# A hand-ordered kernel for RWKV6 attention and a squared-ReLU MoE: a new order, four shared banks, fp32 dummy products

## The chip, the cores and the metric

The kernel runs on one core of one Trainium2 chip. The metric is the device time of one execution in microseconds (us); smaller is better. The core has five engines that work at the same time and are tied by semaphores: TensorE (PE, with its weight loads as PEld), VectorE (DVE), ScalarE (ACT), GpSimd (POOL) and SyncE (SP), which here only issues DMAs. Each engine takes its instructions strictly in the order in which the program gives them.

## The reference

Inputs `r`, `k`, `v`, `w` have shape (4, 8, 768, 48): batch, heads, sequence, head size. `u` is (8, 48), `moe_w_in` is (384, 2048), `moe_w_out` is (2048, 384).

```python
state = zeros((B, H, D, D))
for t in range(S):
    cur   = einsum('bhd,bhe->bhde', u * k[t], v[t])
    y[t]  = einsum('bhd,bhde->bhe', r[t], state + cur)
    state = w[t][..., None] * state + einsum('bhd,bhe->bhde', k[t], v[t])
x   = y.transpose(0, 2, 1, 3).reshape(B * S, H * D)     # (3072, 384)
h   = maximum(x @ w_in, 0)
out = (h * h) @ w_out                                   # (3072, 384)
```

## The kernel before

The 3072 tokens are cut into 12 steps of 256 tokens, three for each of the four sequences. Step `s` does the recurrence for its tokens in two chunks (numbered `c` or 0 and 1) and then the two MoE products for the same tokens.

The attention of a step: `ld` loads w, k, r and v (384 KB each, line 178, on SP's queue). `ww_` (line 264), `kw_` (290) and `rw_` (286) are products with the decay; `lw_` (268) takes a logarithm; `cum_` (324 to 328) sums it on TensorE, `exp_` (340) and `ac_` (346) exponentiate it; `rd_` (358 and 361, always VectorE) makes decayed r and k. Their transposes come from TensorE (`tr_`, line 374, copied by `rkt_`, 389 and 392) for steps 0 to 3 and from DMA (`dtr_`, 401 and 403) for steps 4 to 11. `p_` (420) multiplies them in 64x64 tiles of the array, `pm_` (431 or 434, VectorE) masks the result; `su_` (446), `ts_` (454, 456) and `sn_` (461, POOL) carry the state; `yc_` (493) and `y_` (483) make the output; `ku_` (297), `qp_` (302), `q_` (307), `qs_` and `vs_` (277) and `vq_` (316) make the term with `u`; `ysb_` (504, VectorE) adds all up. `p_`, `su_` and `yc_` use 64x64 tiles of the TensorE array, all other products the whole 128x128 array. `ts_` is a copy for the first chunk of a sequence, on the engine that its word names; for all others it is an addition on VectorE, whatever the word names.

The MoE of a step: `yt_` (516) and `xt_` (521), or a DMA (`dyt_`, 525) from step 6 on, transpose the sum; `m1_` (536) is one of eight parts of the first product, six matmuls of 128x256; `rl_` (545 on ACT, 547 on DVE) is the ReLU, `sq_` (553 or 555) the square; `m2_` (561) is a quarter of the second product for one chunk, four matmuls of 128x384; `os_` (568 or 570) scales, and `store` (574) writes 192 KB. The weights come in eight loads of 768 KB (lines 188 and 194, `ld.g.i` and `ld.g.o`) and `cast` (200) makes them bf16.

The order of everything is the text `ORDER` (lines 17 to 93): one word for one operation, and each engine gets its share of the words in the order in which they stand. `=A`, `=V`, `=G` name ACT, DVE or POOL; `:0`, `:1`, `:m`, `:b` and so on name a PSUM bank. PSUM holds two double banks `att` for the attention, two banks `bk` for the second MoE product and for transposes, and two banks `m1` for the first product. `warm_.n.i` is n dummy products of 128x512 with zeros (line 578), whose result nobody reads.

Of the kernel before, what the change touches and what calls it, by code (L numbers as in the profile page):

```python
# [27 lines left out]
m1_.0.5:0 v_.2=A xt_.1=V qp_.2=G sn_.1.1 m1_.0.4:1 rl_.0.5=A p_.2.1:1 su_.2:b sq_.0.0=A rl_.0.4=V ld.2.o
m1_.1.4:0 cast.i.3=G ts_.2.0=V pm_.2.1 m1_.1.5:1 rl_.1.4=A q_.2 sn_.2.0 m1_.1.3:0 rl_.1.5=A ld.3.o vs_.2.1=G
vs_.2.0=A yc_.2.0:0 yc_.2.1:0 rl_.1.3=V m1_.1.6:1 cast.o.0=G qs_.2=A m1_.1.0:0 ld.3.k rl_.1.6=V sq_.0.2=A  # L30
y_.2:0 rl_.1.0=V m1_.1.1:1 vq_.2=G m1_.1.7:0 rl_.1.1=V ld.3.v m2_.0.1.0:0 sq_.1.2=A rl_.1.7=V sq_.0.1=A
cast.o.1=G m1_.1.2:1 rl_.1.2=A ysb_.2=V m1_.0.7:0 ld.4.w ww_.3=G yt_.2:1 rl_.0.7=V m1_.0.6:1 xt_.2=V m2_.0.1.1
sq_.1.1=A rl_.0.6=V ld.5.w m1_.2.6:0 cast.o.2=G lw_.3 sq_.1.0=A rl_.2.6=A cum_.3:1 sq_.1.3=A rw_.3=G al_.3
ld.5.r m2_.0.0.0:1 m1_.2.7:1 m2_.0.0.1 cast.o.3=V exp_.3 sq_.0.3=A ld.4.k rd_.3.0 kw_.3=G m1_.2.1:0 rl_.2.7=A
ac_.3 m2_.0.1.2 m2_.0.0.2 rl_.2.1=V ku_.3=G m2_.0.0.3 rd_.3.1 ld.4.v m2_.0.1.3 vs_.3.0=A m1_.2.0:1 os_.0.1=V
qp_.3=G ld.5.v m1_.2.3:0 os_.0.0=V rl_.2.0=V tr_.3.1:0 rl_.2.3=A tr_.3.0:1 rkt_.3.1=V v_.3=A ld.4.r m1_.2.4:1
ww_.4=G rkt_.3.0=V m2_.1.0.0:0 rl_.2.4=A q_.3 ww_.5=G p_.3.1:0 vs_.3.1=A ld.6.k su_.3:1 pm_.3.1 p_.3.0:m
m2_.1.0.1 ts_.3.0=A lw_.4 sn_.3.0 ld.5.k pm_.3.0 m2_.1.0.2 qs_.3=A m2_.1.1.0:1 sq_.2.0=A vq_.3=G ts_.3.1=V
m2_.1.0.3 ld.6.w cum_.4:0 m2_.1.1.1 ku_.4=G ac_.4 al_.4 store.0.1 m1_.2.5:0 os_.1.0=A v_.5=A yc_.3.1:1 y_.3:1
lw_.5 kw_.4=G m1_.2.2:1 ld.6.r ysb_.3=V rl_.2.5=A m2_.1.1.2 exp_.4 sn_.3.1 rl_.2.2=V yt_.3:0 rw_.4=G cum_.5:1  # L40
xt_.3=V m2_.1.1.3 vs_.4.0=A ac_.5 sq_.2.1=A qp_.4=G al_.5 m1_.3.0:0 rd_.4.1 v_.4=A m1_.3.3:1 rd_.4.0 dtr_.4.1
m2_.2.0.0:0 rl_.3.0=A rw_.5=G rl_.3.3=A m2_.2.0.1 os_.1.1=V exp_.5 q_.4 dtr_.4.0 su_.4:0 sq_.2.2=A m1_.3.4:0
kw_.5=G rd_.5.0 ww_.6=G m2_.2.1.0:1 rl_.3.4=A ts_.4.0=V sq_.2.3=A m1_.3.5:1 vs_.4.1=A rd_.5.1 sn_.4.0
m2_.2.1.1 store.1.0 ts_.4.1=V rl_.3.5=V ku_.5=G m1_.3.6:0 store.1.1 m2_.2.1.2 qs_.4=A ld.7.w ld.6.v rw_.6=G
p_.4.1:1 rl_.3.6=A p_.4.0:0 pm_.4.1 pm_.4.0 m2_.2.1.3 lw_.6 vq_.4=G m1_.3.1:1 m1_.3.2:0 rl_.3.1=A su_.5:1
dtr_.5.1 dtr_.5.0 vs_.5.1=G sq_.3.0=A rl_.3.2=V yc_.4.0:0 yc_.4.1:0 sn_.4.1 y_.4:0 os_.2.1=V sq_.3.1=A
m1_.3.7:1 ysb_.4=V ld.7.v m2_.2.0.2 rl_.3.7=A ld.8.w kw_.6=G vs_.5.0=G yt_.4:1 ld.7.k sq_.3.3=A m2_.2.0.3
xt_.4=V cum_.6:0 al_.6 m1_.4.4:0 qp_.5=G os_.2.0=A ac_.6 m1_.4.7:1 ts_.5.0=V exp_.6 rl_.4.4=V m2_.3.0.0:1
rl_.4.7=A rd_.6.1 m1_.4.6:0 rd_.6.0 m2_.3.0.1 dtr_.6.1 m2_.3.1.0:0 ku_.6=G qp_.6=G sq_.3.2=A rl_.4.6=A q_.5
dtr_.6.0 p_.5.0:1 p_.5.1:0 vs_.6.0=A m1_.4.5:1 sn_.5.0 m2_.3.0.2 qs_.5=G rl_.4.5=A pm_.5.1 pm_.5.0 vq_.5=G  # L50
m1_.4.1:0 m1_.4.3:1 rl_.4.3=A store.2.1 ld.8.v m2_.3.0.3 rl_.4.1=V ld.8.k v_.6=A ww_.7=G y_.5:0 q_.6 os_.3.0=A
ld.7.r m1_.4.0:1 store.0.0 ld.9.k ww_.8=G yc_.5.0:0 qs_.6=A su_.6:1 yc_.5.1:0 ysb_.5=V vs_.6.1=A ts_.6.0=V
m1_.4.2:0 ld.8.r m2_.3.1.1 rl_.4.0=V yt_.5:1 xt_.5=V sn_.6.0 lw_.7 vq_.6=G rl_.4.2=A p_.6.0:0 m2_.3.1.2
sq_.4.3=A store.2.0 pm_.6.0 m1_.5.2:1 ku_.7=G m1_.5.6:0 ts_.6.1=V yc_.6.1:0 sq_.4.0=A rl_.5.2=A p_.6.1:1
rl_.5.6=A m2_.3.1.3 kw_.7=G pm_.6.1 sq_.4.2=A m1_.5.4:1 rw_.7=G m1_.5.3:0 os_.3.1=V rl_.5.4=A y_.6:0 sn_.6.1
rl_.5.3=A cum_.7:1 kw_.8=G ysb_.6=V al_.7 m2_.4.0.0:1 vs_.7.1=A m1_.5.7:1 m1_.5.5:0 v_.7=G dyt_.6 sq_.4.1=A
rl_.5.7=V qp_.7=G rl_.5.5=V m2_.4.1.0:0 exp_.7 ld.9.w ld.9.v m2_.4.0.1 ac_.7 rd_.7.0 sq_.5.1=A m2_.4.0.2
ku_.8=G rd_.7.1 sq_.5.3=A dtr_.7.0 m2_.4.0.3 m1_.5.0:1 lw_.8 m1_.5.1:0 rw_.8=G rl_.5.0=V su_.7:0 q_.7
rl_.5.1=A cum_.8:1 dtr_.7.1 m1_.6.3:1 qs_.7=A m1_.6.5:0 rl_.6.3=V ld.10.w qp_.8=G ac_.8 sq_.5.0=A m2_.4.1.1
os_.4.0=V ts_.7.0=V ld.11.w sn_.7.0 m1_.6.4:1 rl_.6.5=A al_.8 ww_.9=G m2_.4.1.2 ld.9.r rl_.6.4=V exp_.8  # L60
store.3.0 m2_.5.1.0:1 sq_.5.2=A rd_.8.1 ts_.7.1=V sn_.7.1 m1_.6.0:0 vs_.7.0=G vs_.9.1=A rd_.8.0 m2_.4.1.3
m2_.5.1.1 kw_.9=G rl_.6.0=A dtr_.8.0 p_.7.1:0 v_.8=A p_.7.0:1 vq_.7=G pm_.7.1 m1_.6.1:1 m2_.5.1.2 rl_.6.1=A
pm_.7.0 ku_.9=G m2_.5.1.3 sq_.6.0=A lw_.9 m1_.6.6:0 dtr_.8.1 store.3.1 q_.8 yc_.7.0:0 v_.9=A yc_.7.1:0
rl_.6.6=V rw_.9=G su_.8:1 y_.7:0 os_.5.1=A ts_.8.0=V m1_.6.2:1 ysb_.7=V os_.4.1=A cum_.9:1 m1_.6.7:0 al_.9
dyt_.7 m2_.5.0.0:1 rl_.6.2=V exp_.9 ww_.10=G rl_.6.7=V m2_.5.0.1 ac_.9 ld.10.r rd_.9.1 sq_.6.1=A sq_.6.2=A
sn_.8.0 qp_.9=G ld.10.k qs_.8=G store.4.1 m2_.5.0.2 ld.10.v rd_.9.0 m2_.5.0.3 m2_.6.1.0:0 vs_.8.1=G sq_.6.3=A
dtr_.9.0 vs_.8.0=A p_.8.0:m p_.8.1:0 pm_.8.0 su_.9:1 m2_.6.1.1 ts_.9.0=A pm_.8.1 m2_.6.1.2 lw_.10 m1_.7.4:0
# [564 lines left out]
```

## Time and profile before

| what | value |
|---|---|
| time, median of 3 runs | 182.44 us (182.27 to 183.0) |
| span of the profiled execution, first to last instruction | 182.2 us |
| the profiled execution's own time beside its span | not recorded apart; the lowest run, 182.27 us, stands 0.07 us above the span |
| PE busy | 171.8 us, 94% |
| ACT busy | 132.7 us, 73% |
| DVE busy | 130.0 us, 71% |
| POOL busy | 122.7 us, 67% |
| DMA | 35.81 MB, mean 197 GB/s |

A row of a group reads: line, engine, operation, output tile <- input tiles, shapes, count, then the busy time in us and the mean ns of one. A row of the timeline reads: start in us, duration in us, engine, line and operation, and in square brackets the idle time of the engine ahead of it with what ended it. A row of the chain reads: start, duration, what. A row of the windows reads: window, its length, busy us of PE, PEld, DVE, ACT and POOL with instruction counts in brackets, then the granted clock, the DMA share and GB/s. A matmul's duration in the profile includes its way through the array, so matmuls in a row overlap; their price is the distance between starts, which the chain shows.

### The profile page before, as it was taken

To read this page: it belongs to the slowest core of one execution; us is meant where nothing else is said; L and a number is where in the kernel's file an instruction comes from. 1 tells how busy PE (TensorE), PEld (TensorE's weight loads), DVE (VectorE), ACT (ScalarE), POOL (GpSimd) and SP (SyncE) were. 2 spreads that over 40 slices of the span, in tenths; PEclk is the share of its full clock that TensorE was granted. 3 is DMA by queue.
4 is the path that set the end of the run, shared out by engine and by line. 5 is a ranking of instruction groups with operands and counts; after the bars stand their busy time and mean duration, and the time that the engine had idled before them with its cause. 6 is when DMAs were issued, how large, how long until landed. Compare 5 with 4: busy or idle time off the path is not lost.

```text
span 182.2 us, 5695 instructions
## 1 busy us (share of the span) xinstructions
PE 171.8 (94%) x2385; PEld 123.4 (68%) x2385; DVE 130.0 (71%) x195; ACT 132.7 (73%) x235; POOL 122.7 (67%) x140
## 2 busy tenths in 40 slices
...
GB/s 138 263 263 240 221 359 350 337 314 311 234 274 230 261 158 270 99 247 130 239 296 205 193 270 172 252 189 193 171 109 195 150 47 0 86 144 33 0 86 130
DMA packets 79208, 35.81 MB, mean 197 GB/s; under 512 B 72400, under 2 KB 77648, under 8 KB 79184
## 3 DMA queue, kind: packets, MB, share of 16 engines
...
q8 instruction: 18, 0.29, 0.7%
q14 instruction: 6, 0.05, 0.1%
...
## 4 chain that ended last, share of the span: by engine, by line
PE 75%; SPq 10%; DMA 8%; ACT 4%; issue 1%; DVE 1%; ACTq 0%
PE bk L561 32%; PE m L536 32%; SPq L178 8%; DMA w_st<-in_moe_w_in_dram 5%; PE att L420 3%; DMA rT<-rdec_buf 2%; PE att L483 2%; PE att L493 2%; PE att L446 1%; ACT gt L545 1%; PE att L326 1%; ACT wi_sb L200 1%; PE bk L516 1%; SPq L188 1%; SPq L205 1%
## 5 line engine op out<-in xcount | busy, mean ns | idle before, releaser
L536 PE MATMUL m<-xT,wi_sb 128*128 128x256 bf16 x576 | 74.0, 273 | 1.3 <-ACT gt L545 1.2
L561 PE MATMUL bk<-wo_sb,gt 128*128 128x384 bf16 x384 | 71.9, 326 | 0.0
L536 PEld LDWEIGHTS <-wi_sb 128*128 128x128 bf16 x576 | 54.8, 98 | 13.0 <-issue 0.9
L561 PEld LDWEIGHTS <-gt 128*128 128x128 bf16 x384 | 36.9, 98 | 19.2
L545 ACT ACTIVATE gt<-m 128x512 f16<-128x512 f32 x56 | 33.0, 595 | 22.3 <-PE m L536 21.9
L553 ACT ACTIVATE gt<-gt 128x1024 bf16<-128x1024 f16 x42 | 43.3, 1051 | 1.4 <-DVE gt L547 1.1
L547 DVE TENSOR_SCALAR gt<-m 128x512 f16<-128x512 f32 x40 | 27.0, 686 | 9.6 <-PE m L536 9.3
L434 DVE TENSOR_TENSOR pmT<-att,mask 128x1024 bf16<-128x1024 f32 x20 | 23.9, 1218 | 4.5 <-PE att L420 4.5
L297 POOL TENSOR_TENSOR ku<-k_raw,u_bc 128x768 f32<-128x768 f32 x12 | 21.8, 1819 | 0.2 <-DMA u_bc<-in_u_dram 0.2
L302 POOL TENSOR_TENSOR ku<-ku,r_raw 128x768 f32<-128x768 f32 x11 | 20.7, 1881 | 0.2
L316 POOL TENSOR_TENSOR ku<-v_sh,qs 128x768 f32<-128x768 bf16 x11 | 16.3, 1479 | 4.9 <-ACT qs L277 4.8
L277 ACT CAST v_sh<-v_raw 64x384 bf16<-64x384 f32 x34 | 17.3, 508 | 0.4
L290 POOL TENSOR_TENSOR k_raw<-k_raw,w_raw 128x384 f32<-128x384 f32 x12 | 12.2, 1013 | 6.4 <-DMA k_raw<-in_k_dram 6.3
L286 POOL TENSOR_TENSOR r_raw<-r_raw,w_raw 128x384 f32<-128x384 f32 x12 | 12.0, 1000 | 6.4 <-DMA r_raw<-in_r_dram 6.4
L504 DVE TENSOR_TENSOR y_sb<-att,ku 128x768 bf16<-128x768 f32 x12 | 11.4, 953 | 5.5 <-issue 1.6
L461 POOL TENSOR_TENSOR S<-t_state,ac_buf 128x192 bf16<-128x192 f32 x20 | 10.2, 512 | 6.4 <-DVE t_state L456 3.4
L361 DVE TENSOR_TENSOR kdec_buf<-k_raw,att 128x768 bf16<-128x768 f32 x12 | 11.4, 949 | 3.4 <-ACT att L340 2.8
L358 DVE TENSOR_TENSOR rdec_buf<-r_raw,att 128x384 bf16<-128x384 f32 x24 | 12.1, 547 | 2.2 <-ACT att L340 1.1
L340 ACT ACTIVATE att<-att 128x768 f32<-128x768 f32 x12 | 9.6, 798 | 3.1 <-PE att L328 1.9
L568 ACT ACTIVATE o_sb<-bk 128x384 f32<-128x384 f32 x13 | 6.3, 485 | 7.4 <-PE bk L561 7.3
L307 DVE TENSOR_REDUCE q<-ku 128x16 f32<-128x768 f32 x12 | 11.3, 943 | 0.0
L578 PE MATMUL att<-warm 128*128 128x512 bf16 x27 | 9.1, 492 | 1.2 <-DVE half_ones L228 1.2
...
## 6 DMA issues: line engine op xcount, KB each, us to landing
...
rT<-rdec_buf SPq DMA_TRANSPOSE x16, 4.1
```

The lines of the kernel that those rows point to most:

```text
L178: nc.sync.dma_start(out=t[:, hs, at:at + 2, :].rearrange("p h j d -> p h (j d)"), in_=src[b, hs, i * T:(i + 1) * T, :].rearrange("h (p j) ...
L277: copy(out[j * Q:(j + 1) * Q, c], src[c * Q:(c + 1) * Q, :, j])
L290: tensor_mul("kw_", s, h)(raw["k", s][:, hs, 0, :], raw["k", s][:, hs, 1, :], raw["w", s][:, hs, 1, :])
L297: tensor_mul("ku_", s, h)(tiles["ku", s][:, hs], raw["k", s][:, hs, 1:3, :], u_bc[:, hs, None, :].to_broadcast([C, n, 2, D]))
L302: tensor_mul("qp_", s, h)(ku, ku, raw["r", s][:, heads(h), 0:2, :])
L316: tensor_mul("vq_", s)(vq[:], tiles["vs", s][:], tiles["qs", s][:, :, :, None].to_broadcast([C, 2, H, D]))
L434: nc.vector.tensor_mul(pmT, ps_p[:].rearrange("p e (x t) -> p (e x) t", t=C), mk.to_broadcast([C, 8, C]))
L536: nc.tensor.matmul(ps1[:, j, :], wi_sb[:, n // 4, kk, n % 4 * 128:(n % 4 + 1) * 128], tiles["xT", s][:, :, kk, :], start=(kk == 0), stop=( ...
L545: nc.scalar.activation(rl, m1, AF.Relu, scale=RS)
L547: nc.vector.tensor_scalar(out=rl, in0=m1, scalar1=RS, scalar2=0.0, op0=ALU.mult, op1=ALU.max)
L553: nc.scalar.activation(gt, rl, AF.Square)
L561: nc.tensor.matmul(m2, gt[:, n, c * C:(c + 1) * C], wo_sb[:, n, :], start=(n == 0), stop=(n == NT - 1))
```

## The change

Three things change.

1. `ORDER` is written anew. The loads now come as w, k, r, v of step 0, then w, k, r of step 1, `u`, v of step 1, w of step 2, two loads of `moe_w_in`, and then r and k of step 2. The first MoE parts of steps 0 and 1 stand ahead of most of step 2's attention. On TensorE the parts of `p_` and `yc_` of one step are more often apart, with MoE parts between them. Engines are named anew: over the whole kernel `sq_` has 17 words on V instead of 6, `rl_` 32 instead of 40, `kw_` 6 instead of 0, `rw_` 3 instead of 0, `ww_` 4 instead of 2, `ku_` 3 instead of 0, `qp_` 5 instead of 1, `vq_` 5 instead of 1, `vs_` 7 instead of 0, `v_` 1 instead of 0, `xt_` 4 instead of 6, `os_` 9 instead of 11 and `rkt_` 4 instead of 5. The number of loads, stores, matmuls of the real work and DMA transposes stays.
2. The four single banks become one list, `quad`. `m1_` and `m2_` may each use any of the four. The quarters of `m2_` may come in any order: the first to run starts the sum and the last to run ends it.
3. The zeros of the dummies become fp32, and there are 12 of them instead of 46.

The core of the diff, with the opening of `ORDER` up to `yt_.2` in the old and the new form (the rest of the order is left out):

```diff
-ld.0.w ld.0.k ld.0.r ld.0.u ld.1.w ww_.0=V lw_.0 warm_.11.5 cum_.0:0 kw_.0=G exp_.0 rd_.0.1 ld.0.v warm_.8.5
-tr_.0.1:0 rkt_.0.1=A ld.1.k ld.1.r rw_.0=G ld.2.w ku_.0=G rd_.0.0 ld.1.v warm_.3.5 tr_.0.0:1 ww_.1=V
-rkt_.0.0=A qp_.0=V ld.2.r v_.0=A warm_.5.5 p_.0.0:m p_.0.1:1 ac_.0 lw_.1 q_.0 su_.0:b ld.2.k cum_.1:0
-ts_.0.0=A kw_.1=G pm_.0.0 pm_.0.1 vs_.0.0=A sn_.0.0 ld.1.i exp_.1 rw_.1=G vs_.0.1=A qs_.0=A rd_.1.1 ku_.1=G
-warm_.3.2 yc_.0.1:1 ld.0.i ac_.1 ts_.0.1=V rd_.1.0 warm_.2.2 tr_.1.1:0 sn_.0.1 y_.0:1 rkt_.1.1=A vq_.0=V
-tr_.1.0:1 ww_.2=G ld.2.i v_.1=A rkt_.1.0=V ysb_.0=V vs_.1.1=A warm_.4.2 p_.1.1:0 qp_.1=G su_.1:m ld.2.v
-pm_.1.1 lw_.2 yt_.0:0 cum_.2:1 ld.3.i ts_.1.0=V rw_.2=G q_.1 exp_.2 kw_.2=G xt_.0=V vs_.1.0=A rd_.2.0 qs_.1=G
-ac_.2 cast.i.1=A rd_.2.1 warm_.10.1 tr_.2.0:1 sn_.1.0 p_.1.0:0 ku_.2=G ts_.1.1=V yc_.1.1:1 tr_.2.1:0
-cast.i.0=A pm_.1.0 ld.0.o m1_.0.3:0 ld.3.w rkt_.2.1=V m1_.0.2:1 vq_.1=G rkt_.2.0=V y_.1:1 rl_.0.3=A yc_.1.0:1
...
+ld.0.w ww_.0=V lw_.0 warm_.5.4 cum_.0:0 ld.0.k kw_.0=G exp_.0 rd_.0.1 ld.0.r rw_.0=G ac_.0 rd_.0.0 warm_.2.5
+tr_.0.1:2 ld.0.v rkt_.0.1=A v_.0=G tr_.0.0:1 rkt_.0.0=V vs_.0.1=A ld.1.w ww_.1=G lw_.1 su_.0:m p_.0.1:b
+pm_.0.1 vs_.0.0=A p_.0.0:1 pm_.0.0 ld.1.k cum_.1:0 exp_.1 kw_.1=G rd_.1.1 ld.1.r rw_.1=G rd_.1.0 ts_.0.0=A
+sn_.0.0 ld.0.u ku_.0=V qp_.0=V q_.0 ku_.1=G qp_.1=G ts_.0.1=A sn_.0.1 warm_.2.0 tr_.1.1:2 rkt_.1.1=A qs_.0=G
+vq_.0=G yc_.0.1:1 y_.0 ac_.1 tr_.1.0:0 rkt_.1.0=A warm_.1.1 p_.1.0:b pm_.1.0 p_.1.1:0 ld.1.v v_.1=A pm_.1.1
+q_.1 vs_.1.1=A warm_.1.3 su_.1:b ysb_.0=V yc_.1.0:0 ld.2.w ww_.2=V warm_.1.3 yt_.0:3 xt_.0=V vs_.1.0=G
+ts_.1.0=A ld.1.i cast.i.1=A sn_.1.0 ld.0.i ts_.1.1=A y_.1 m1_.0.3:1 yc_.1.1 m1_.0.2:2 qs_.1=A lw_.2 cum_.2:1
+cast.i.0=G m1_.0.1:3 vq_.1=V ysb_.1=V rl_.0.2=A yt_.1:2 xt_.1=V rl_.0.3=V exp_.2 ld.2.r rw_.2=G rd_.2.0 ld.2.k
+m1_.0.0:0 kw_.2=G rd_.2.1 rl_.0.1=A m1_.1.0:3 rl_.0.0=A rl_.1.0=A m1_.1.1:1 rl_.1.1=A sq_.1.0=A sn_.1.1 ld.2.i
+ac_.2 ld.2.v sq_.0.0=A tr_.2.0:3 rkt_.2.0=V cast.i.2=V ku_.2=G v_.2=G tr_.2.1:0 rkt_.2.1=V qp_.2=V ld.3.i
+m1_.1.3:3 rl_.1.3=A m1_.1.4:1 vs_.2.0=G ld.1.o su_.2:0 p_.2.0:1 ts_.2.0=V vs_.2.1=A cast.i.3=G m1_.0.4:2
+sn_.2.0 m1_.1.2:3 p_.2.1:0 ld.0.o m1_.1.5:0 ld.3.w pm_.2.0 rl_.1.4=A rl_.0.4=A m1_.0.5:2 ld.2.o sq_.0.1=A
+ld.3.o m1_.1.6:1 rl_.1.2=V yc_.2.1:1 pm_.2.1 y_.2 rl_.0.5=A sq_.1.1=V m1_.0.6:3 rl_.1.6=V cast.o.1=G m1_.1.7:1
+ld.3.k cast.o.0=G rl_.1.5=V yc_.2.0 rl_.0.6=V q_.2 m1_.0.7:0 sq_.1.2=A m2_.0.1.1:3 m2_.0.1.0 m2_.1.1.1:2
+ld.3.r ww_.3=G qs_.2=A cast.o.3=G rl_.0.7=V m2_.0.0.1:0 cast.o.2=A lw_.3 rl_.1.7=V sq_.0.2=V vq_.2=V m2_.1.1.0
+ysb_.2=V sq_.0.3=V m2_.0.0.0 m2_.0.0.2 yt_.2:1 xt_.2=V ku_.3=G cum_.3:1 al_.3 qp_.3=G m2_.1.1.2 sq_.1.3=A
...
+    quad = bk + m1_bank
...
-    warm = consts.tile([C, 512], BF16)
+    warm = consts.tile([C, 512], FP32)
...
-        ps1 = tiles["m1", s, g] = m1_bank[int(slot["m1_", s, g])][:].rearrange("p (j t) -> p j t", j=2)
+        ps1 = tiles["m1", s, g] = quad[int(slot["m1_", s, g])][:].rearrange("p (j t) -> p j t", j=2)
...
+    summed = {}
+
     def m2_(s, c, q):
         gt = tiles["gt", s]
-        m2 = bk[int(slot["m2_", s, c])][:, 0:DM]
-        for n in range(4 * q, 4 * q + 4):
-            nc.tensor.matmul(m2, gt[:, n, c * C:(c + 1) * C], wo_sb[:, n, :],
-                             start=(n == 0), stop=(n == NT - 1))
+        m2 = quad[int(slot["m2_", s, c])][:, 0:DM]
+        summed[s, c] = summed.get((s, c), 0) + 1
+        for n in range(4):
+            nc.tensor.matmul(m2, gt[:, 4 * q + n, c * C:(c + 1) * C], wo_sb[:, 4 * q + n, :],
+                             start=(summed[s, c] == 1 and n == 0), stop=(summed[s, c] == NT // 4 and n == 3))
...
-            nc.tensor.matmul((bk + m1_bank)[i][:] if i < 4 else att[i - 4][:, 0, :], warm[:, 0:C], warm[:],
+            nc.tensor.matmul(quad[i][:] if i < 4 else att[i - 4][:, 0, :], warm[:, 0:C], warm[:],
                              start=True, stop=True)
```

128 lines of the change are left out of this document (60 added, 68 removed).

## The prediction

> **What bounds the kernel now.** I read the page first, then the windows, the waits of PE, the chain of work that ended last, and last the timeline of DVE in the opening.
>
> ```profile
> span 182.2 us, 5695 instructions
> PE 171.8 (94%) x2385; PEld 123.4 (68%) x2385; DVE 130.0 (71%) x195; ACT 132.7 (73%) x235; POOL 122.7 (67%) x140
> PE 75%; SPq 10%; DMA 8%; ACT 4%; issue 1%; DVE 1%; ACTq 0%
> ```
>
> PE holds three quarters of the chain. Which stretch that is, the windows show (PE, PEld, DVE, ACT, POOL busy):
>
> ```profile
> 42.00:118.60 76.60, 76.05 (x1161) 56.05 (x1159) 63.01 (x96) 65.42 (x117) 66.57 (x70) 1.00 1.10 224
> 100.00:120.00 20.00, 20.00 (x334) 14.54 (x333) 18.20 (x29) 15.74 (x28) 18.14 (x24) 1.00 1.25 228
> ```
>
> From 42 us on PE is busy without a gap (76.05 of 76.60) while DVE is busy 82% of that stretch, and 91% in its fullest 20 us here. PE's own waits are small:
>
> ```profile
> PE m L536 <- ACT gt L545: 1.2, 1, 1.2
> PE att L420 <- DMA rT<-rdec_buf: 0.6, 2, 0.4
> ```
>
> The first MoE product starts here, in PE's timeline:
>
> ```profile
> 26.99 1.47 PE L536 MATMUL m<-xT,wi_sb 128*128 128x256 bf16 x12
> ```
>
> So the kernel is a gapless PE behind an opening of some 27 us with little real PE work in it. The change can win in the opening only, and it can lose in two ways: by more PE time, or by an engine that no longer keeps ahead of PE. The chain gives PE's prices as distances between starts, and three marks in time:
>
> ```profile
> 42.00 0.34 PE bk L516 x6
> 53.63 0.26 PE att L446 x32
> 59.20 0.66 PE m L536 x6
> 59.86 0.65 PE bk L561 x4
> 64.37 0.37 PE att L446 x32
> 64.74 0.76 PE m L536 x6
> 118.58 0.51 PE att L483 x16
> 178.91 0.49 ACT o_sb L568
> ```
>
> The first row is `yt_.2`, the transpose of step 2's sum; the seventh is `y_` of step 8; the last is the last `os_`, after which the store takes the rest of the 182.2 us. A `su_` inside a block of 64x64 work takes 0.26; one that comes straight after a 128x128 product takes 0.37; and an `m1_` after such a block takes 0.76 instead of 0.66. Each block of 64x64 work (a run of `p_`, `su_`, `yc_` with nothing else between) thus costs 0.11 at its entry and 0.10 at its exit, about 0.22 us, whatever is in it.
>
> **The change part by part.** I split the time at `yt_.2`, which waits for `ysb_.2` on DVE in both orders.
>
> (a) The opening, by DVE's queue. Its rows:
>
> ```profile
> 7.73 0.95 DVE L361 TENSOR_TENSOR kdec_buf<-k_raw,att 128x768 bf16<-128x768 f32 x1 [2.60 <-ACT att L340]
> 20.34 0.94 DVE L504 TENSOR_TENSOR y_sb<-att,ku 128x768 bf16<-128x768 f32 x1
> 21.20 1.21 DVE L434 TENSOR_TENSOR pmT<-att,mask 128x1024 bf16<-128x1024 f32 x1
> 33.80 0.69 DVE L547 TENSOR_SCALAR gt<-m 128x512 f16<-128x512 f32 x1 [0.82 <-PE m L536]
> 37.78 1.29 DVE L547 TENSOR_SCALAR gt<-m 128x512 f16<-128x512 f32 x2 [0.43 <-PE m L536]
> 39.42 1.35 DVE L547 TENSOR_SCALAR gt<-m 128x512 f16<-128x512 f32 x2 [0.35 <-PE m L536]
> 40.68 0.95 DVE L504 TENSOR_TENSOR y_sb<-att,ku 128x768 bf16<-128x768 f32 x1
> ```
>
> The last row is `ysb_.2`, done at 41.63; `yt_.2` follows at 42.00. From the first row (`rd_.0.1`) on, DVE's 41 instructions up to there last 31.9 us by their group means; neighbours overlap by 0.07 (0.94 us long, but 20.34 to 21.20 between starts), so 29.0 us without gaps, against 33.9 that passed. DVE idled 4.8 us, 1.6 of it in the three waits for `m1_` shown. In the new order DVE has ahead of `ysb_.2` the same kinds and counts and in addition one `ku_`, one `qp_`, one `vq_`, one `cast`, two `sq_`, and a `pm_` in two halves instead of whole:
>
> ```profile
> L302 DVE TENSOR_TENSOR ku<-ku,r_raw 128x768 f32<-128x768 f32 x1 | 0.9, 945 | 0.0
> L316 DVE TENSOR_TENSOR ku<-v_sh,qs 128x768 f32<-128x768 bf16 x1 | 1.7, 1683 | 0.0
> L200 DVE CAST wo_sb<-w_st 128x1536 bf16<-128x1536 f32 x1 | 1.0, 1031 | 0.1
> L555 DVE TENSOR_TENSOR gt<-gt 128x1024 bf16<-128x1024 f16 x6 | 4.3, 732 | 5.8 <-ACT gt L545 5.7
> L434 DVE TENSOR_TENSOR pmT<-att,mask 128x1024 bf16<-128x1024 f32 x20 | 23.9, 1218 | 4.5 <-PE att L420 4.5
> L431 DVE TENSOR_TENSOR pmT<-m,mask 128x512 bf16<-128x512 f32 x8 | 5.1, 684 | 2.0 <-ACT v_sh L277 1.3 <-PE m L420 0.7
> ```
>
> That is 2 x 0.945 (`ku_` has `qp_`'s shape) + 1.683 + 1.031 + 2 x 0.732 + (2 x 0.684 - 1.218) = 6.2 us, less seven overlaps of 0.07: 5.7 us. DVE now runs behind PE, so I let the three waits for `m1_` go (-1.6) and keep the other 3.2 us of idling. `yt_.2` comes **4.1 us later**, at 46.1. Bounds: -4.8 + 5.7 = +0.9 if DVE never idles, +5.7 if it idles as before.
>
> (b) PE work that is done by then. Ahead of `yt_.2` stand 16 `m1_` and 7 `m2_` instead of 15 and 1: 0.66 + 6 x 0.65 = **4.6 us** less remain after it.
>
> (c) Blocks. After `yt_.2` the new order has 34 blocks of 64x64 work instead of 19, because the two `p_` and the two `yc_` of a step mostly stand apart: 15 x 0.22 = **+3.3 us** of PE time, all of it in the gapless part.
>
> (d) DVE between `yt_.2` and `y_.8`. PE took 76.6 us (42.00 to 118.58). The new order has there 9 `m2_`, 3 `m1_` and one `su_` less and 7 blocks more: 76.6 - 5.9 - 2.0 - 0.3 + 1.5 = 70.0 us. DVE has 100 instructions there, 72.6 us by the group means (before 66.9 with 93), 65.6 with the overlaps. `vs_` on DVE has no row; I price its halves of 384 elements at 0.42, between these:
>
> ```profile
> L456 DVE TENSOR_TENSOR t_state<-S,att 128x192 f32<-128x192 bf16 x12 | 4.2, 346 | 1.4 <-POOL S L461 1.2 <-PE att L446 0.3
> L521 DVE COPY xT<-bk 128x768 bf16<-128x768 bf16 x6 | 3.3, 552 | 1.7 <-PE bk L516 1.6
> ```
>
> DVE would have to be at work 94% of the time and never wait; it was at work 82% before. At the 91% of its fullest window it needs 72.1 us, so PE waits **2.0 us**. Bounds: nothing (94% is kept) and 80.0 - 70.0 = 10 us (82%). After `y_.8` DVE's need falls below PE's, and I take nothing.
>
> (e) The dummies. No row has an fp32 product. These rows bound it:
>
> ```profile
> 1.19 4.87 PE L578 MATMUL att<-warm 128*128 128x512 bf16 x11 [1.19 <-DVE half_ones L228]
> 5.85 0.29 PE L324 MATMUL att<-half_ones,lw_buf 128*128 128x2 bf16 x4
> 6.60 2.14 PE L578 MATMUL att<-warm 128*128 128x512 bf16 x8
> 5.22 0.52 ACT L268 ACTIVATE lw_buf<-ww 128x384 bf16<-128x384 f32 x1 [2.17 <-DVE ww L264]
> ```
>
> Eleven bf16 dummies end just as `lw_.0` does (5.74), and `cum_.0` starts at 5.85. If an fp32 dummy costs as much as a bf16 one, the new first five take 5/11 of 4.66 us and delay nothing. If twelve fill the time of 46 (3.83 old ones each), the five are 19 old ones: 11 until 5.85, 8 more in 2.14, and `cum_.0` starts near 8.1, 2.2 us late, with all of DVE's chain behind it. I take 0, by the row of the same shape, and keep +2.2 for the range. The Trainium skill, "FP8 and Floating Point Precision", section "TensorE Precision Notes", says that a true fp32 product makes four passes through the array; no run shows it yet. By that rule the five are 20 old ones, and the sum would be 2.4 us higher (rival 1).
>
> (f) Weights and loads. These rows show when loads landed:
>
> ```profile
> 10.25 0.77 DVE L264 TENSOR_TENSOR ww<-w_raw 128x384 f32<-128x384 f32 x1 [0.63 <-DMA w_raw<-in_w_dram]
> 11.75 0.83 ACT L272 CAST v_bf<-v_raw 128x768 bf16<-128x768 f32 x1 [0.25 <-DMA v_raw<-in_v_dram]
> 28.55 1.47 ACT L200 CAST wi_sb<-w_st 128x1536 bf16<-128x1536 f32 x1 [1.84 <-DMA w_st<-in_moe_w_in_dram]
> 30.67 1.46 POOL L200 CAST wi_sb<-w_st 128x1536 bf16<-128x1536 f32 x1 [2.40 <-DMA w_st<-in_moe_w_in_dram]
> ```
>
> A 384 KB load takes about 1.5 us (10.25 to 11.75). `ld.0.i` moves ahead of two of them on SP's queue and lands near 25.5 instead of 28.55; `ld.2.i` has the same fourteen loads ahead and lands at 30.7 as before. I cost the gain at nothing beyond (b), because the DVE work ahead of `yt_.2` is the later input. The r and k of step 2 pay for it: they land near 28.5. `rd_.2` cannot start on DVE before about 29.9 by the count in (a), which hides them with some 0.4 us to spare; without that cover each costs up to 1.5.
>
> (g) The rest. Any bank for `m1_` and `m2_` can give back PE's 1.2 us wait for a bank at most, and that wait lies in the opening that (a) already counts: 0. The order of the `m2_` quarters: 0, the same matmuls. ACT and POOL lose work to DVE; neither held PE, so 0. The transposes by DMA keep their number; where one is issued later, PE waits for it, as the 0.6 us row shows, and SP's loads behind it wait too; those loads run a step ahead, so I take 0. At the end four stores instead of two follow each other into the last 3 us; 0, with the last store's 2.8 us (179.4 to 182.2) as now.
>
> Sum against the span: 182.2 + 4.1 - 4.6 + 3.3 + 2.0 = 187.0. The median stands 0.24 above the span: **187.3 us**. Differences under 0.5% (0.9 us) cannot be told from none here (the three runs lie 0.7 us apart).
>
> **The rivals.** 1. *The first dummies hold back the opening*: (e) at its upper side, 187.3 + 2.4 = 189.7. For it: fp32 values are twice as wide, and `cum_.0` has only 0.1 us of slack. Against it: no row. 2. *DVE becomes the bound outright*: in the middle it gets no denser than its 82%, 10 us instead of 2: 195.3. For it: it waits for PE's `m1_` and `p_` in order, as in the rows of (a). Against it: when DVE is late, what it waits for is ready. 3. *Faster: DVE is never starved*, in the opening and behind it. Then `yt_.2` comes 0.9 later instead of 4.1, and (d) is 0: 187.3 - 3.2 - 2.0 = 182.1, and PE's 0.6 us of DMA waits behind it and 0.3 of slack may go too: 181.2. It counts as faster only if DVE idles less than about 0.3 us up to `ysb_.2`, against 4.8 now. For it: the weights come earlier, and four banks let PE run ahead. Against it: `pm_`, `rl_`, `rd_`, `ysb_` and `ts_` all wait for another engine's result, in DVE's fixed order. 4. *No effect*: the banks and the order move nothing that ends last, and the earlier weights just pay for the blocks: 182.4.
>
> **How the numbers follow.** Forecast 0.55 (its own range 184.5 to 189.0), rival 1 0.20, rival 2 0.10, rival 3 0.10, rival 4 0.05. Slower holds the first three: 0.85; same 0.05; faster 0.10. The range runs from the no-idle bound (182.1, rounded up to 182.5) to halfway between rivals 1 and 2, 193.0; it leaves out most of rivals 2 to 4.
>
> **What would show it.** Blocks: `m1_` of 0.76 in the chain 15 times more, PE's busy time about 3 us up apart from the dummies. (a): `yt_.2` near 46 us. (d): DVE over 90% busy in the middle, PE with waits for DVE (`pm_`, `ysb_`, `rd_`) where it had none. (e): the start of `cum_.0`, 5.9 or 8. The prediction is wrong if `yt_.2` comes before 43 us, if the blocks hide under waits, or if PE waits for DVE in the middle by much more than 2 us.

## The result and the profile after

The changed kernel takes 200.42 us (median of 4 runs, 198.7 to 201.67) against 182.36 us (181.98 to 183.0) for the kernel before on the same chip: a ratio of 1.0989 with a 95% interval of 1.0949 to 1.1029, 18.1 us slower. The forecast was 187.3 us, the upper end of its range 193.0. The sign was right, the size was not, and the range did not hold the time.

The head of the page of the changed kernel, and its windows (columns as before; the first window runs from `yt_.2` to `y_.8`):

```profile
span 198.0 us, 5647 instructions
PE 179.2 (91%) x2363; PEld 123.3 (62%) x2363; DVE 162.3 (82%) x232; ACT 117.0 (59%) x211; POOL 107.7 (54%) x129
```

```profile
52.33:124.62 72.29, 70.57 (x1071) 50.42 (x1072) 68.63 (x100) 50.12 (x91) 46.87 (x59) 1.00 0.80 174
100.00:120.00 20.00, 19.59 (x277) 14.04 (x274) 19.55 (x31) 14.68 (x24) 11.20 (x17) 1.00 0.83 167
140.00:160.00 20.00, 15.69 (x201) 9.71 (x202) 17.07 (x24) 8.41 (x17) 9.93 (x8) 1.00 0.62 140
```

DVE went from 130.0 to 162.3 us of work. It is busy for 95% of the stretch from `yt_.2` to `y_.8` (68.63 of 72.29) and for 98% of the fullest 20 us, while ACT and POOL are at 59% and 54% over the span. Behind that stretch, in the 20 us from 140 on, PE stands still for 4.3 us. The waits of PE name the same engine (us in total, times, longest):

```profile
PE att L421 <- DVE t_state L457: 2.7, 1, 2.7
PE m L582 <- DVE t_state L457: 2.2, 1, 2.2
PE bk L517 <- DVE y_sb L505: 2.0, 2, 1.1
PE att L447 <- DVE kdec_buf L362: 1.6, 1, 1.6
```

In the kernel before, no wait of PE for DVE was above 1.2 us in sum. The same three marks that the prediction used, from the timeline of PE and, for the last, of ACT:

```profile
52.33 0.51 PE L517 MATMUL bk<-ident,y_sb 128*128 128x128 bf16 x6 [1.14 <-DVE y_sb L505]
124.62 0.56 PE L484 MATMUL att<-v_sh,pmT 128*128 128x48 bf16 x16
...
194.74 0.49 ACT L572 ACTIVATE o_sb<-m 128x384 f32<-128x384 f32 x1 [5.36 <-PE m L565]
```

| stretch | before | forecast | after |
|---|---|---|---|
| start to `yt_.2` | 42.00 | 46.1 | 52.33 |
| `yt_.2` to `y_.8` | 76.58 | 72.0 | 72.29 |
| `y_.8` to the last `os_` | 60.33 | 65.6 | 70.12 |

(The forecast's last figure is 60.33 plus what its parts move there: 76.6 + 60.3 - 4.6 + 3.3 = 135.6 us of PE work after `yt_.2`, less the 70.0 of the middle.) So 6.2 us went missing in the opening and 4.5 behind `y_.8`; the middle came out as forecast.

What ends PE's 2.71 us wait at 157.69 is read from the chain (start, duration, what):

```profile
155.98 0.47 DVE att L334
156.45 0.46 DVE k_raw L291
156.91 0.47 DVE o_sb L574
157.38 0.27 DVE t_state L457
157.65 0.04 issue
157.69 0.43 PE att L421 x16
```

The `ts_` of step 10 (L457) stands in DVE's queue behind an `al_`, a `kw_` and an `os_`, none of which it needs, and PE's `p_` behind it.

The opening shows why DVE is late. In the timeline of DVE, and beside it in that of POOL:

```profile
9.50 0.95 DVE L362 TENSOR_TENSOR kdec_buf<-k_raw,att 128x768 bf16<-128x768 f32 x1 [4.44 <-ACT att L341]
17.72 1.21 DVE L298 TENSOR_TENSOR ku<-k_raw,u_bc 128x768 f32<-128x768 f32 x1
18.96 2.45 DVE L303 TENSOR_TENSOR ku<-ku,r_raw 128x768 f32<-128x768 f32 x1
29.12 1.91 DVE L317 TENSOR_TENSOR ku<-v_sh,qs 128x768 f32<-128x768 bf16 x1
37.70 2.18 DVE L303 TENSOR_TENSOR ku<-ku,r_raw 128x768 f32<-128x768 f32 x1
42.94 1.23 DVE L556 TENSOR_TENSOR gt<-gt 128x1024 bf16<-128x1024 f16 x1
47.94 0.85 DVE L556 TENSOR_TENSOR gt<-gt 128x1024 bf16<-128x1024 f16 x1
48.71 2.57 DVE L317 TENSOR_TENSOR ku<-v_sh,qs 128x768 f32<-128x768 bf16 x1
```

```profile
18.18 2.41 POOL L303 TENSOR_TENSOR ku<-ku,r_raw 128x768 f32<-128x768 f32 x1
37.61 1.46 POOL L201 CAST wi_sb<-w_st 128x1536 bf16<-128x1536 f32 x1
48.32 2.14 POOL L303 TENSOR_TENSOR ku<-ku,r_raw 128x768 f32<-128x768 f32 x1
```

A `qp_` (L303) takes 2.45 and 2.18 us; the prediction priced it at 0.945, from one row. Both inputs lie in SBUF, and POOL reads SBUF at the same time: beside the first it runs a product of its own, beside the second a cast of weights. A `qp_` of POOL that runs beside a `vq_` of DVE is lengthened as well: the kernel before had one such row, which the prediction did not use (timeline of POOL, before; the mean of this group is 1.88):

```profile
18.95 2.55 POOL L302 TENSOR_TENSOR ku<-ku,r_raw 128x768 f32<-128x768 f32 x1
```

This gave the theory that the experiments test: **VectorE and GpSimd hold each other up when both read SBUF, a VectorE instruction with two inputs there, and the change moved such instructions to VectorE while GpSimd kept on reading.** The rivals: VectorE merely has too much work (37 instructions more); the blocks of 64x64 work cost more than 0.22 us; the dummies set back the whole chain; the order is at fault whatever the engines.

### The profile page after: what moved, and what is told of

Read it like the earlier page. It is cut to its first block, busy times and chain, and to the rows that moved or that the text cites. A ratio compares the mean times of both kernels' runs of the same rounds, so it can differ in the third digit from the quotient of the medians.

```text
span 198.0 us, 5647 instructions
## 1 busy us (share of the span) xinstructions
PE 179.2 (91%) x2363; PEld 123.3 (62%) x2363; DVE 162.3 (82%) x232; ACT 117.0 (59%) x211; POOL 107.7 (54%) x129
## 5 line engine op out<-in xcount | busy, mean ns | idle before, releaser
L537 PEld LDWEIGHTS <-wi_sb 128*128 128x128 bf16 x576 | 54.0, 98 | 13.2 <-issue 2.9
L537 PE MATMUL bk<-xT,wi_sb 128*128 128x256 bf16 x318 | 42.5, 273 | 2.5 <-DVE t_state L457 1.6
L565 PE MATMUL m<-wo_sb,gt 128*128 128x384 bf16 x208 | 39.1, 326 | 0.1
L537 PE MATMUL m<-xT,wi_sb 128*128 128x256 bf16 x258 | 34.5, 273 | 0.1
L554 ACT ACTIVATE gt<-gt 128x1024 bf16<-128x1024 f16 x31 | 32.2, 1052 | 3.0 <-DVE gt L548 2.8
L565 PE MATMUL bk<-wo_sb,gt 128*128 128x384 bf16 x176 | 32.8, 326 | 0.0
L546 ACT ACTIVATE gt<-m 128x512 f16<-128x512 f32 x33 | 19.4, 594 | 13.1 <-PE m L537 12.7
L546 ACT ACTIVATE gt<-bk 128x512 f16<-128x512 f32 x31 | 18.3, 595 | 11.1 <-PE bk L537 10.8
L435 DVE TENSOR_TENSOR pmT<-att,mask 128x1024 bf16<-128x1024 f32 x18 | 21.4, 1214 | 0.1
L548 DVE TENSOR_SCALAR gt<-bk 128x512 f16<-128x512 f32 x22 | 14.8, 683 | 5.3 <-PE bk L537 5.3
L556 DVE TENSOR_TENSOR gt<-gt 128x1024 bf16<-128x1024 f16 x17 | 16.0, 948 | 0.1
L303 POOL TENSOR_TENSOR ku<-ku,r_raw 128x768 f32<-128x768 f32 x7 | 13.6, 1945 | 3.8 <-DVE ku L298 3.5
L362 DVE TENSOR_TENSOR kdec_buf<-k_raw,att 128x768 bf16<-128x768 f32 x12 | 11.3, 945 | 5.1 <-ACT att L341 5.1
L308 DVE TENSOR_REDUCE q<-ku 128x16 f32<-128x768 f32 x12 | 11.3, 943 | 2.6 <-POOL ku L303 2.6
```

Of the source, the lines that this page charges most:

```text
L303: tensor_mul("qp_", s, h)(ku, ku, raw["r", s][:, heads(h), 0:2, :])
L435: nc.vector.tensor_mul(pmT, ps_p[:].rearrange("p e (x t) -> p (e x) t", t=C), mk.to_broadcast([C, 8, C]))
L537: nc.tensor.matmul(ps1[:, j, :], wi_sb[:, n // 4, kk, n % 4 * 128:(n % 4 + 1) * 128], tiles["xT", s][:, :, kk, :], start=(kk == 0), stop=( ...
L546: nc.scalar.activation(rl, m1, AF.Relu, scale=RS)
L548: nc.vector.tensor_scalar(out=rl, in0=m1, scalar1=RS, scalar2=0.0, op0=ALU.mult, op1=ALU.max)
L554: nc.scalar.activation(gt, rl, AF.Square)
```

## The experiments

Times are medians of 4 runs (of 10 for the kernel before with fills); "excess" is the median less that of the kernel before on the same chip (182.4 to 183.3). The changed kernel has an excess of 18.1. The 95% intervals of the ratios are worth 0.4 to 1.8 us to each side, most of them 0.6 to 1.1, so a difference of less than about 1.5 us between two rows is not told apart from none. The kernel of the contention ran once. The diffs show a few of the changed words; the others are left out.

### Order and engine names apart

Edit 1: the new order, banks and dummies, every `=engine` as the kernel before has it. Edit 2: the old order, with the engine names of the new one.

```diff
 # edit 1
-ysb_.1=V rl_.0.2=A yt_.1:2 xt_.1=V rl_.0.3=V exp_.2 ld.2.r rw_.2=G rd_.2.0 ld.2.k
+ysb_.1=V rl_.0.2=V yt_.1:2 xt_.1=V rl_.0.3=A exp_.2 ld.2.r rw_.2=G rd_.2.0 ld.2.k
 # edit 2
-cast.i.0=A pm_.1.0 ld.0.o m1_.0.3:0 ld.3.w rkt_.2.1=V m1_.0.2:1 vq_.1=G
+cast.i.0=G pm_.1.0 ld.0.o m1_.0.3:0 ld.3.w rkt_.2.1=V m1_.0.2:1 vq_.1=V
```

> The new order, its banks and its fp32 dummies, but each operation on the engine that the old order names. Theory A (the loss comes from the work that moved to VectorE, by its amount and by the lengthening of VectorE's products with two SBUF inputs while GpSimd works): VectorE's busy time falls from 162 to about 130 us, its product of 128x768 no longer takes 1.6 us, and the time falls from 200 to 190 or less. Theory B (the loss comes from the order of the work on TensorE and its blocks): the time stays at 196 or more.

> The old order, banks and bf16 dummies, but each operation on the engine that the new order names. Theory A: the loss comes along with the engines: 192 us or more, VectorE busy near 160 us. Theory B: 186 us or less.

Edit 1 took 223.8 us (ratio 1.2232, 1.2199 to 1.2265), edit 2 208.35 (1.1393, 1.1374 to 1.1412): both are slower than either kernel. The page of the first, and the longest row of waits of the second:

```profile
PE 187.9 (84%) x2363; PEld 127.9 (57%) x2363; DVE 132.6 (60%) x197; ACT 131.5 (59%) x235; POOL 123.7 (56%) x140
```

```profile
ACT gt L540 <- PE m L531: 47.9, 34, 3.7
```

With the old names DVE's work is back at 132.6 us, and the kernel is 23 us slower than with the new ones. Taken by the letter, the first expectation came out for theory B and the second for theory A (DVE has 158.4 us of work there). As I read it, each order is fitted to its own engines: an instruction put on another engine stands there in a queue that was not laid out for it. ACT's ReLUs wait 47.9 us for PE, against 21.9 us in the kernel before; but a PE that is late for another reason would show the same, so this reading is not shown. The two parts do not add, and this pair decides nothing between the theories, except that an order can be slow with little work on DVE.

### The dummies

In the new order bf16 dummies, 11, 8, 8, 4, 4 and 4 of them instead of 5, 2, 2, 1, 1 and 1; and in the kernel before fp32 dummies, 5, 2, 1, 1, 1, 1, 1 and 2 instead of 11, 8, 3, 5, 3, 2, 4 and 10.

```diff
-    warm = consts.tile([C, 512], FP32)
+    warm = consts.tile([C, 512], BF16)
-ld.0.w ww_.0=V lw_.0 warm_.5.4 cum_.0:0 ld.0.k
+ld.0.w ww_.0=V lw_.0 warm_.11.4 cum_.0:0 ld.0.k
```

> The changed kernel with bf16 dummies: 11, 8, 8, 4, 4, 4 in the places of 5, 2, 2, 1, 1, 1 in fp32. If the first five fp32 dummies hold back the opening, the first sum on TensorE starts near 5.9 us instead of 8.0 and the time falls by 1 to 2 us; if the opening is set by VectorE's queue behind it alone, the time stays within 0.5 us of the changed kernel's.

> The kernel before with fp32 dummies in its own places: 5, 2, 1, 1, 1, 1, 1, 2 for 11, 8, 3, 5, 3, 2, 4, 10. If an fp32 dummy takes four times a bf16 one, the first sum on TensorE starts near 8.0 us and the time rises by 1.5 to 2.2 us; if the opening has slack behind it, by less than 0.9 us.

The changed kernel with bf16 dummies took 199.06 us, excess 16.0 (ratio 1.09, 1.0839 to 1.0961). The kernel before with fp32 dummies took 185.27, excess 2.1 (1.0137, 1.0083 to 1.0191). PE's timeline of the changed kernel, then of the one with bf16 dummies:

```profile
1.45 6.71 PE L582 MATMUL att<-warm 128*128 128x512 f32 x10 [1.45 <-DVE half_ones L229]
8.00 0.24 PE L325 MATMUL att<-half_ones,lw_buf 128*128 128x2 bf16 x4
...
8.42 1.88 PE L582 MATMUL att<-warm 128*128 128x512 f32 x4
```

```profile
5.80 0.25 PE L320 MATMUL att<-half_ones,lw_buf 128*128 128x2 bf16 x4 [0.36 <-ACT lw_buf L264]
...
6.24 1.89 PE L577 MATMUL att<-warm 128*128 128x512 bf16 x8
```

Two fp32 products (four rows: each shows as two) take 1.88 us, eight bf16 ones 1.89: one fp32 product costs four. The Trainium skill, "FP8 and Floating Point Precision", section "TensorE Precision Notes", says four passes; the trace agrees. `cum_.0` starts at 8.00 instead of 5.80. Of these 2.2 us about 2 reach the end of either kernel (the second pair of dummy kernels, below, says 1.7); at `yt_.2` 1.3 of them are left, for it starts at 51.00 with bf16 dummies and at 52.33 without.

### Long VectorE work, or GpSimd beside it

The products of the attention (`ku_`, `qp_`, `vq_`, `ww_`, `kw_`, `rw_`) are replaced by constant fills, which read nothing: first VectorE's 26, then GpSimd's 46, then both, and as a control those of GpSimd in the kernel before. There they are 68, not the 56 of the expectation. The diff is that of GpSimd's; for VectorE's it asks for "V".

```diff
     def tensor_mul(*op):
+        if where[key(*op)] == "G":
+            return lambda out, x, y: nc.gpsimd.memset(out, 0.9)
         return nc.vector.tensor_mul if where[key(*op)] == "V" else nc.gpsimd.tensor_mul
```

> The changed kernel, but the 26 products of fp32 tiles that it has on VectorE (kw, rw, ww, ku, qp, vq) are left out: each writes a constant into its output instead, without reading. Theory A (VectorE's load holds TensorE): VectorE's busy time falls by about 14 us and the time falls by 8 us or more, to 192 or less. Theory B (the order of TensorE's work): 197 or more.

> The changed kernel, but the 46 products of fp32 tiles that it has on GpSimd are left out: each writes a constant instead, without reading. VectorE keeps every instruction. If GpSimd's reads lengthen VectorE's products, VectorE's mean for sq falls from 948 to about 730 ns, for qp from 1600 to about 950, its busy time by 6 to 9 us, and the time falls by 4 us or more. If the lengthening does not matter for the end, the time stays within 1.5 us.

> The changed kernel with all 72 products of fp32 tiles on VectorE and GpSimd left out (constants written instead). With GpSimd's alone left out the time was 191.5 us. If VectorE's load still holds TensorE there, the time falls by another 4 us, to about 187; what is then left above 183 us is the fp32 dummies and the blocks. If it stays at 190 or more, the order of TensorE's work holds the rest.

> The control: the kernel before with its 56 products on GpSimd left out (constants written instead). It has few VectorE instructions with two SBUF inputs and a TensorE without gaps: the time stays within 2 us of the kernel before. If it falls by 6 us or more, GpSimd's products cost any kernel of this kind that much, and the fall of the changed kernel says nothing on its VectorE.

| filled | us | excess | ratio, interval | DVE busy | POOL busy |
|---|---|---|---|---|---|
| none | 200.42 | 18.1 | 1.0989 (1.0949 to 1.1029) | 162.3 | 107.7 |
| VectorE's | 195.81 | 12.5 | 1.0674 (1.0619 to 1.0729) | 151.0 | 103.8 |
| GpSimd's | 191.51 | 8.2 | 1.0432 (1.0379 to 1.0486) | 152.4 | 66.1 |
| both | 189.42 | 6.6 | 1.0379 (1.032 to 1.0438) | 146.2 | 63.9 |
| GpSimd's, kernel before | 183.02 | 0.2 | 1.0014 (0.998 to 1.0048) | 129.2 | 68.6 |

The groups of DVE of the changed kernel (busy, mean ns, idle before), then of the one with GpSimd's products filled, whose DVE instructions are the same:

```profile
L556 DVE TENSOR_TENSOR gt<-gt 128x1024 bf16<-128x1024 f16 x17 | 16.0, 948 | 0.1
L303 DVE TENSOR_TENSOR ku<-ku,r_raw 128x768 f32<-128x768 f32 x5 | 8.0, 1600 | 0.1
L291 DVE TENSOR_TENSOR k_raw<-k_raw,w_raw 128x384 f32<-128x384 f32 x6 | 5.5, 918 | 0.0
```

```profile
L558 DVE TENSOR_TENSOR gt<-gt 128x1024 bf16<-128x1024 f16 x17 | 12.3, 726 | 0.1
L305 DVE TENSOR_TENSOR ku<-ku,r_raw 128x768 f32<-128x768 f32 x5 | 5.3, 1053 | 0.1
L293 DVE TENSOR_TENSOR k_raw<-k_raw,w_raw 128x384 f32<-128x384 f32 x6 | 3.5, 576 | 0.0
```

Nothing on DVE was changed, and its work fell by 9.9 us and the time by 9.8. A square falls from 948 to 726 ns, a `qp_` from 1600 to 1053, while the groups of DVE with an input in PSUM keep their means (`pm_` 1214 and 1216 ns, the `rd_` of k 945 and 946). At the marks of the prediction this run has `yt_.2` at 48.11, `y_.8` at 119.36 and the last `os_` at 185.95: of the 8.8 us that the span lost, 4.2 lie in the opening, 1.0 in the middle and 3.5 behind `y_.8`.

The same edit in the kernel before, where few such instructions stand on DVE, gains nothing, though it takes 54 us of work from POOL. So a lighter POOL is worth nothing by itself there; in the new order it cannot be wholly excluded as a part of the 9.8. Filling VectorE's own products after that takes another 1.6, which is little more than the intervals allow to tell; filled first, they take 5.6, and GpSimd's then 5.9. What the two share is counted to whichever goes first. The forecasts for VectorE's products alone (192 or less, or 197 or more) and for both (near 187, or 190 or more) left gaps, and 195.81 and 189.42 fell into them. The amount of work that DVE loses does not set the gain: 11.3 us less brought 5.6 with VectorE's products filled, 9.9 us less brought 9.8 with GpSimd's.

### The contention by itself

A kernel of its own runs one kind of VectorE instruction 8 times alone, 12 times while GpSimd runs fp32 products of 128x768 without pause, and 12 times while GpSimd only fills (the diff shows the core).

```diff
+    def two_in():
+        nc.vector.tensor_mul(d_out[:], d_in[0][:], d_in[1][:])
+    def from_psum():
+        nc.vector.tensor_mul(h_out[:], ps[:], m_in[:])
+    def pool_mul():
+        nc.gpsimd.tensor_mul(p_out[:], p_in[0][:], p_in[1][:])
+    def pool_set():
+        nc.gpsimd.memset(p_out[:], 0.5)
```

> A kernel of its own that computes nothing of the reference: four VectorE operations (fp32 product of two SBUF tiles 128x768; square 128x1024 of fp16; product of a PSUM and an SBUF tile 128x1024; copy 128x768 fp32 to bf16), each 8 times alone, 12 times beside GpSimd products of two SBUF tiles, and 12 times beside GpSimd fills. If GpSimd's reads hold back VectorE's second input: the first two operations take 1.5 to 2.5 times as long beside products and the same beside fills; the product from PSUM does not change. If the memory as a whole is the limit, all four are slower beside both.

Its timeline, DVE (start, us in all, line, count), but for the products of two SBUF inputs, the squares and the casts beside GpSimd's products:

```profile
22.00 7.91 DVE L51 TENSOR_TENSOR d_out<-d_in,d_in 128x768 f32<-128x768 f32 x8
...
59.31 11.88 DVE L51 TENSOR_TENSOR d_out<-d_in,d_in 128x768 f32<-128x768 f32 x12
...
103.32 8.68 DVE L54 TENSOR_TENSOR h_out<-h_in 128x1024 bf16<-128x1024 f16 x12
...
125.47 15.05 DVE L57 TENSOR_TENSOR h_out<-ps,m_in 128x1024 bf16<-128x1024 f32 x12
143.15 15.06 DVE L57 TENSOR_TENSOR h_out<-ps,m_in 128x1024 bf16<-128x1024 f32 x12
...
188.57 11.63 DVE L60 CAST h_out<-d_in 128x768 bf16<-128x768 f32 x12
```

Those three by line, with the ns of one (shortest, median, longest) and the first and last start; L63 is GpSimd's product in the first of them:

```profile
L51 DVE TENSOR_TENSOR d_out<-d_in,d_in x12: 957/2438/2441, 32.6 to 56.8; 128x768 f32<-128x768 f32 x12
L63 POOL TENSOR_TENSOR p_out<-p_in,p_in x10: 1802/2394/2601, 30.7 to 52.6; 128x768 f32<-128x768 f32 x10
L54 DVE TENSOR_TENSOR h_out<-h_in x12: 677/2172/2174, 80.4 to 101.7; 128x1024 bf16<-128x1024 f16 x12
L60 DVE CAST h_out<-d_in x12: 560/2039/2040, 166.6 to 186.5; 128x768 bf16<-128x768 f32 x12
```

Of each twelve, nine run beside a product of GpSimd; the first starts ahead of GpSimd's, and the last two run after its tenth has ended and take as long as alone. So the product of two SBUF inputs takes 0.96 us alone, 2.44 beside a product of GpSimd and 0.96 beside fills; the fp16 square 0.69, 2.17 and 0.69; the product with one input in PSUM 1.22 each time; the cast from fp32 to bf16 0.56, 2.04 and mostly 1.05 beside fills. A product of GpSimd takes 1.80 alone and 2.39 beside VectorE's products. The two forecasts did not name this outcome whole: the first two operations are 2.5 and 3.1 times as long, where 1.5 to 2.5 was expected, and the cast, with one SBUF input, is slowed as well. The Trainium skill, "SBUF — State Buffer", section "Who interferes with whom", says that a VectorE instruction with two SBUF inputs contends with a GpSimd instruction that reads SBUF and not with one that only writes it, and that copies and casts in a two-port mode contend with any: all four series agree, though no trace names the mode of the cast.

### The squares on ScalarE

Nothing is left out here: the 17 squares that DVE has in the changed kernel (6 in the kernel before) go to ACT.

```diff
-rl_.0.5=A sq_.1.1=V m1_.0.6:3 rl_.1.6=V
+rl_.0.5=A sq_.1.1=A m1_.0.6:3 rl_.1.6=V
```

> The changed kernel with its 17 squares of VectorE on ScalarE, where each takes 1.05 us; nothing is left out. VectorE loses 16 us, ScalarE reaches 135 us, as in the kernel before. If VectorE's load is what holds TensorE, the time falls by 5 us or more; if ScalarE's order of work takes its place, by less than 2 us or not at all.

197.0 us, ratio 1.0749 (1.065 to 1.0848): some 4 us faster than the change as it is, with the order unaltered and DVE at 146.0 us. The forecasts were 5 us or more, or less than 2; this lies between. The runs spread from 195.46 to 198.56, so the gain is known to about 2 us. It takes back a part of DVE's load and does not reach the kernel before.

### GpSimd's casts on ScalarE

The other way to thin out GpSimd's reads: its 16 words `v_` and `vs_` (24 instructions) go to ACT.

```diff
-ld.0.v rkt_.0.1=A v_.0=G tr_.0.0:1
+ld.0.v rkt_.0.1=A v_.0=A tr_.0.0:1
```

> The changed kernel with the 16 casts of v that GpSimd did (8 whole, 8 in halves) on ScalarE, which is busy 59% of the span. VectorE keeps all its instructions. If GpSimd's reads lengthen VectorE's products, VectorE's busy time falls by 2 us or more and the time falls by 2 us or more; if only the number of VectorE's instructions counts, its busy time stays within 0.5 us and the time within 1 us.

204.66 us, excess 21.6 (ratio 1.1172, 1.111 to 1.1233): 3.6 slower than the change. The instructions on DVE did get shorter (`kw_` from 918 to 641 ns, `qp_` from 1600 to 1352), but DVE's sum fell by 2.5 us only, and PE now waits for the casts, which stand in ACT's queue (waits of PE; this row is about half of the 3.6 us, the rest was not traced):

```profile
PE att L442 <- ACT v_bf L268: 1.7, 3, 0.8
```

So less contention is not enough where something that PE waits for moves back.

### The blocks of 64x64 work

In the old order 17 MoE parts were moved in between `p_`, `su_` and `yc_`, so that 39 blocks stand after the first MoE product instead of 22. In the new order 11 parts were moved together, 28 blocks instead of 39; and the same with all products filled.

```diff
-p_.4.1:1 rl_.3.6=A p_.4.0:0 pm_.4.1 pm_.4.0 m2_.2.1.3 lw_.6
+p_.4.1:1 rl_.3.6=A m2_.2.1.3 p_.4.0:0 pm_.4.1 pm_.4.0 lw_.6
```

```diff
-p_.4.0:1 m2_.2.0.0:1 pm_.4.0 p_.4.1:m sq_.3.1=A
+p_.4.0:1 p_.4.1:m m2_.2.0.0:1 pm_.4.0 sq_.3.1=A
```

> The kernel before, with one part of the MoE products (by one to three places in TensorE's order) moved in between neighbouring parts of the 64x64 work, 17 times: 39 blocks of 64x64 work after the first MoE product instead of 22, as in the new order; nothing else moves. If a block costs 0.22 us on a TensorE without gaps, the time rises by 3.7 us (2%); if the entry and the exit hide, it stays within 0.9 us.

> The changed kernel, with 11 parts of the 64x64 work moved by one to three places to stand next to their neighbours: 28 blocks instead of 39. If blocks count in full, the time falls by 2.4 us; if TensorE's waits for VectorE take up what is gained, by less than 1 us.

> All 72 fp32 products left out, and 28 blocks of 64x64 work instead of 39, by the same moves that made the changed kernel 1.8 us slower. If blocks cost 0.22 us each wherever TensorE does not wait, the time falls by 2.4 us against 189.4; if the moved parts wait for their inputs here too, it does not fall.

Splitting the old order cost 6.35 us (189.64; ratio 1.0327, 1.0291 to 1.0362). By 0.22 each, 17 blocks come to 3.7, and PE's busy time from the first MoE product on did rise by 3.7 us (from 149.9 to 153.7 in the windows). The rest is near the wait that PE got (its waits; 0.2 in the kernel before):

```profile
PE bk L510 <- DVE y_sb L498: 2.5, 3, 1.1
```

Merging in the new order gained nothing: 202.24, excess 18.9 (1.1032, 1.0981 to 1.1082), not told apart from the change; with the products filled 192.18, excess 9.0, which is 2.5 worse than without the merging. The waits of PE in the first of these say why:

```profile
PE att L416 <- DVE rdec_buf L354: 2.4, 2, 1.4
PE m L416 <- DVE o_sb L569: 1.2, 1, 1.2
```

A `p_` that is moved ahead stands before DVE has made its input or emptied its bank. So the blocks have a price where PE never waits, and the new order pays it and in exchange does not wait there. What the 15 extra blocks cost the new order in time, by themselves, was not isolated.

### What is left without either cause

All products filled, and bf16 dummies.

```diff
-        return nc.vector.tensor_mul if where[key(*op)] == "V" else nc.gpsimd.tensor_mul
+        return lambda out, x, y: (nc.vector if where[key(*op)] == "V" else nc.gpsimd).memset(out, 0.9)
-    warm = consts.tile([C, 512], FP32)
+    warm = consts.tile([C, 512], BF16)
```

> All 72 fp32 products left out (constants written), as in the run that took 189.4 us, and bf16 dummies as in the run with those alone. If the dummies' delay is paid in full once VectorE is unloaded, the time falls by 1.5 to 2.2 us; if VectorE's queue in the opening hid it, by less than 0.9 us.

188.04 us, excess 4.9 (ratio 1.0266, 1.0235 to 1.0297), 1.7 less than with fp32 dummies. Its page and PE's timeline:

```profile
span 186.2 us, 5666 instructions
```

```profile
46.80 0.50 PE L512 MATMUL bk<-ident,y_sb 128*128 128x128 bf16 x6
...
116.62 0.56 PE L479 MATMUL att<-v_sh,pmT 128*128 128x48 bf16 x16
```

`yt_.2` starts at 46.80 (forecast 46.1), and the stretch to `y_.8` takes 69.8 us, where the forecast had 70.0 of PE work. With the two mis-priced causes gone, (a), (b) and (c) alone give 182.2 + 4.1 - 4.6 + 3.3 = 185.0, against a span of 186.2. This is agreement, not proof: the filled products also take work from DVE that the forecast counted. The sum of (b) and (c) can be seen by itself: PE's busy time from `yt_.2` on is 135.3 us, where 136.2 before, less 4.6, plus 3.3 gives 134.9.

The excess of 18.1 thus divides, in this order of removal, into 9.8 for GpSimd's reading products, 1.6 for VectorE's own, 1.7 for the dummies, and 4.9 that stay with the order, its blocks included. With VectorE's products filled first, the first two are 5.6 and 5.9. Of the 4.9, the profiles show where they lie: `yt_.2` starts 4.8 us later than before (46.80 against 42.00), and the stretch from there to the end is 0.8 shorter (139.4 against 140.2). What holds the opening there stays open. No kernel of this study beat the one before.

## Why the prediction was wrong, step by step

**What bounds it: right.** PE held the chain with next to no waits, and the change could lose by more PE work or by an engine that fell behind. It lost mostly by the second, on DVE.

**(a) The opening: right in its method, the sum 6.2 us short.** This is the step that failed. DVE's first `rd_` starts at 9.50 instead of 7.73, 1.8 us late by the dummies, of which 1.3 are left at `yt_.2`. Then its instructions up to `ysb_.2` were longer than priced; the idling, kept at 3.2 us, was not the error (its five gaps of 0.24 to 0.71 us make 2.8). Seven instructions, in the rows above, make 4.7 us: (2.45 + 2.18 - 2 x 0.945) + (1.91 + 2.57 - 2 x 1.683) + (1.23 + 0.85 - 2 x 0.732) + (1.21 - 0.945). With GpSimd's products filled the opening is 4.2 us shorter. The price of `qp_` and `ku_` came from one row in which POOL happened not to read: the single `qp_` on DVE of the kernel before ran while POOL stood idle. A price from one row is the price under that row's neighbours. The `vq_` at 1.683 was such a price the other way round: with GpSimd's products filled, that instruction of the kernel before takes 0.95. Two rows of the same size and kind of work at 0.945 and 1.683 stood in the same fence; the difference between them was the sign.

**(b) and (c): borne out as PE work.** The split kernel in the old order shows 3.7 us of PE work for 17 blocks, with PE waits on top, and PE's work from `yt_.2` on came within 0.4 us of the forecast. The new order showed no way to take the blocks back.

**(d) The middle: 72.1 forecast, 72.3 measured, by two errors that cancel.** DVE's work was 68.6 us instead of 65.6, again by the mis-priced instructions, but DVE was 95% busy instead of the 91% that I took as the most it would reach. "After `y_.8` I take nothing" failed by 4.5 us: a `ts_` or `rd_` that PE needs stands in DVE's queue behind other work, and PE waited 2.71 and 1.60 us for it, though DVE was not full there (17.07 of 20 us). Of the 4.5, 3.5 went when GpSimd's products were filled.

**(e) The dummies: the wrong end taken.** Rival 1 was true as a mechanism, with `cum_.0` at 8.00 as its row had it (8.1). It brought about 2 us of the 2.4. I took nothing, by the row of the same shape, although its type differed.

**(f), (g): no run contradicts them,** and none was made for them alone.

**From span to time.** I put the median 0.24 us above the span. The profiled execution of the changed kernel took 200.15 us with a span of 198.0, 2.15 above; further executions of the kernel before stand about 1.8 above theirs. The profile that the prediction rests on had a longer span (182.2) than any of those (180.2 to 182.1), which hid the difference. That is 1.9 us of the miss.

In sum: 6.2 (opening) + 0.3 (middle) + 4.5 (behind `y_.8`) + 1.9 (span to time) + 0.3 (the median over the profiled execution) = 13.2, against 200.4 - 187.3 = 13.1.

**The rivals.** Rival 2 (DVE outright the bound, 195.3) was nearest in place and size, but by another mechanism: DVE did not get stuck at 82%, it got denser and its instructions longer. The chance of 0.10 for it was too low, because its only price was one of waiting, and none of the ranges held a longer instruction. (Halfway between rivals 1 and 2 is 192.5, not 193.0; the time lies outside of either.)
